# Attention into a mixture of attention experts on one core: v's blocks in pairs, q/k products by halves, a bound on loads, a new order

## The chip, the core and the metric

The kernel runs on one core of a Trainium2 chip. The metric is the device time in microseconds, from the first to the last instruction and what lies around it; several runs are made and the median is told. Five engines work side by side: TensorE (PE: matmuls; PEld: its weight loads), VectorE (DVE), ScalarE (ACT), GpSimd (POOL) and SyncE (SP), which here only issues DMAs. TensorE writes to eight PSUM banks of 512 fp32 columns; VectorE and ScalarE read them out.

## The reference

For 8 batches of 8 heads, 576 tokens and a head size of 64:

```python
kv  = einsum('bhsd,bhse->bhde', k, v)          # 64 x 64 a head, no softmax
out = einsum('bhsd,bhde->bhse', q, kv)
x   = out / sqrt(mean(out*out, -1) + 1e-6) * g_norm   # then heads side by side: 576 x 512
logits = x @ w_gate                             # 4 experts, the best 2 kept
w = softmax over the kept two
for e in range(4):                              # head size 64
    q, k, v = x @ wq[e], x @ wk[e], x @ wv[e]
    a = causal softmax(q @ k.T / 8)
    y += w[:, e] * (a @ v @ wo[e])              # zero where e isn't kept
```

## The kernel before

Each batch goes through the same steps, and eight batches are interleaved. A step is a named task (name, batch, index); `emit` maps names to functions:

- `lk`, `lv`, `lq` load k, v and q; k and v come in four pieces a batch (256 or 320 KB), q in two (576 KB). `lw`, `lwo` load weights, `ws`, `wo` bring them into their final type. `st` stores a block of the result.
- `kv` (L400) multiplies k and v, `kvc`, `kvx` bring the result into SBUF, `qc` transposes q (L423), `o` (L436) multiplies both. `oc` and `sq` copy and square o, `ms` (L468) sums squares, `ln`, `rs`, `na`, `nb`, `lo` (L487 to L506) make the reciprocal root, `bc` (L549) spreads it over the heads, `xm` (L557) multiplies it in: x, transposed, in `xT`.
- `G`, `L`, `lt` and the small tasks to `gate` choose the experts and their weights.
- `qp`, `kp` (`proj`, L629) multiply x by wq and wk for a pair of experts: two halves of 288 tokens into two banks, which one copy (`qpc`, `kpc`) brings out as 576 columns. `v` (L609) does one block of 128 tokens, 256 columns of one bank; `vc` copies it.
- `sc` (L659), `exp` (L671), `msk` (L678) make the weights of attention, `pv` (L704) multiplies them with v, `rc`, `iv`, `oc2` scale (L732), `ot` (L747) transposes, `y` (L777) is the last product, four matmuls of 256 columns a block; `yc` copies it to a stage buffer.

The order of the 1086 tasks is written out by hand as a string, `ORDER`, two characters a task. Two further strings give each task's engine (`ENGINE`) and the banks or buffers that it takes (`SLOTS`). Every engine and every DMA queue runs its tasks in that order. `place` hands out slots, `big` two banks, `small` one; `use` makes an instruction wait for other engines' work on its bank. `ZEROS` puts products of zeros (L812) ahead of some tasks at the start, so that TensorE is busy while the first loads come. All loads and, but for one task, all stores are issued on SyncE's queue, and a DMA there also waits for the eighth before it, whose semaphore it takes over.

```python
ZEROS = {
    ("kv", 0, 2): 31, ("kv", 0, 0): 14, ("o", 0, 0): 3,
}
```

Of the kernel before, what the change touches and what calls it, by code (L numbers as in the profile page):

```python
# [17 lines left out]
RUN, LO = 9, 4  # L18

# [6 lines left out]
    ("kv", 0, 2): 31, ("kv", 0, 0): 14, ("o", 0, 0): 3,  # L26
# [15 lines left out]
    "6PBJAEC+9u8IBKCy9VEqAFBMCzBN9xD4D5BLD6F4EuEv8H9X8G9YEwD8AIExAGDCDADDD7DBEy9+ACF1D9AH9Z9rADDE9sBU8J2OF3DFAM6X6Y"
    "DGBV9f8KC9DHBeBfEzDIBcE+9a8L9z8M9hBmF2CABnF0DJBdBW9b9y9c80E-6U9iBk6VBlBXC7DLC881DWBoDQDXALAJ9gDS8NDTDRDKBpBwDM"
    "Bs8OBxDUAKBtDVF6F54SFDDN6ZF7F8FBDOBuANBvFCA0F9AOFE8bA1BiA2APDsA3BqFAAQDPBYCDBj8cDtCBFFCC8PDYA46R8QCEEDBZ8SBaCJ"
    "Br6S6TC0DqA58TFGFHFIEBBzEEECDgByBgARDrFJB+FKCFDbBbBhFTFRASFLCGFUCMFSCHFM6QDyFX8R6WDZB-DaCIFNDzDhFOC1FPELDcFYCN"
    "CLC2DwC3EJEMC48YDxATEK8ZDmFQDd8UAUDnCKDuFVFWDvEFC58VC6COAWFrCPCQEGAX8WFsFtFl2RDoFuCRFmFvE0EREHD+CSDpCTD-EPE38a"
    "2LAcFwEIAVFZEOGIGJFcDkAYDlE2CaCUAdFa4PAZCbCVDiGKCgE1DjAeAa8dE4CcDeF-EQENGLCWFzFbChGQG0FdFxF+DfFy8XE52UFjFkFhG1"
    "E6FeESE7G2FfG3E84YGSGRGTCi4MFiGOAbFgETGMEUEVGNCdG6E9GWGYGUCeEWCXGPFnGVGXEAFpGZG7FoEXG8CYEeEfEYG5FqCfG9GaGEG4Gb"
    "EZCZEgGcEbGFGdGhEcGeEhEaEiGfGAEdGiGBGCGoGgGlGjGpGDGmEjGGGkGrGHGuGxGqGsGnGvGtGyGwGz"
)  # L50
ENGINE = (
    "SSSSSSSSSSGGVSASVSASVSVSVSVSAVVVVAAGAGAVAAAVVVVVVVAAAVAAAVAAAVVVAAAVVVGVVVVVVVVVVVVVGAGGVVGVAVAVAVVVAVVVVVAVAV"
    "AVAGGGGGVVGVVVVAVAVAVAVAVAGGGGGVVGVVAVVSVASVASVASSSSSSSSSSSVVVVAGGGAVVVVVVAGAAVAAGVAAAVVVVVVVGVVVVVVVVVGAVGVVG"
    "VAVAVAVVVVVAVVVAVAVAVAGGGGGVVGVVAVVVVVAVAVAVAGGGGGVVGVVAVVSVVSVASVASVASSSSSSSSSSSVVVVAVGGAVVVVVVVGAGAGVAVAAAVV"
    "VGVVVGVVVVVVVVVGAVGVVGVAVVVAVVVAVVVAVAVAVAVAGGGGGVVGVVAVAVVVAVAVAVAGGGGGVVGVVVVVSVVSVVSVVSSSSSSSSSSSVVVVVGVGGV"
    "VVVVVAGVAAAVGVAAAVVVVVVVGVVVVVVVVVGAGGVVGVVVVVAVAVVVVVAVAVAVAVAGGGGGVVGVVVVVVAVAVAVAVAGGGGGVVGVVAVVSVVSVVSVVSV"
    "ASSSSSSSSSSSVVVVAVAAVVVVVVVAGVGAGVGVAAAVVVVVVVGVVVVVVFVVGAVGVVGVAVAVVVAVAVVVVVAVAVAVAGGGGGVVGVVVVAVVVAVAVAVAGG"
    "GGGVVGVVVVASVASVASVVSSSSSSSSSSSVVVVVAAVAVVVVVVAGVGVGAAVAAAVVVGVVVGVVFVFVVVVGAGGVVGVAVAVVVAVVVAVAVAVAVAVAGGGGGV"
    "VGVVVVAVVVAVAVAVAGGGGGVVGVVVVASVVSVASVVSVVSSSSSSSSSSSVVVVAGGGVVVVVVVVAAGVAAAVAAAVVVGVVVVFVFVVVFVVGAVGVVGVAVAVV"
    "VAVVVAVAVAVAVAVAGGGGGVVGVVVVAVVVAVAVAVAGGGGGVVGVVVVASVASVASVASSSSSSSSSSSVVVVAAGVGVVVVVVVGVGAAAAVAAAVVVGVVVGVVV"  # L60
    "VVVVVVGAVGVVGVVVAVAVAVVVAVAVAVAVAVAGGGGGVVGVVVGVVAVVVAVAVAVAVAVAGGGGGVVGVVVGVVVVVVASVASVASVASVAC"
)
SLOTS = (
    "00001112345101674500134123201451672334401235601561201301150675341670015023016767230145607231601245236701452310"
    "16745101234200015603470156123456017012306745101236700145001016723401231415640167235012367454123010456723456701"
    "10014532671423014567013200456712450345110234510670234510672301452306101234567230014256000751546721234267010567"
    "06120045673074506701234856701452367014235601456011023041156722306945067234567106723450167234560123670011451670"
    "2310145016235A67B012235101134675013467501230456702390B451267301234506806745067340125011673660B0453567019456712"
    "301067023450001123637024509250113704253023502983530573"
# [13 lines left out]
def names(nb):  # L83
# [3 lines left out]
    for b in range(nb):  # L87
# [12 lines left out]
        out += [(m, b, i) for i in r5 for m in ("v", "vc")]  # L100
        for p in r2:
            out += [(m, b, p) for m in ("qp", "qpc", "kp", "kpc")]
# [3 lines left out]
        out += [(m, b, i) for i in (r5 if b % 2 else r4) for m in ("y", "yc", "st")]  # L106
# [14 lines left out]
def kernel(  # L121
# [37 lines left out]
    begun = [0]  # L159

# [154 lines left out]

    def load(m, dst, src, b, p, z):
        n, t0 = LO + z, LO * z
        hs = slice(4 * p, 4 * p + 4)
        rows = src[b, hs].rearrange("h (r t) d -> r h (t d)", t=RUN)[:, :, t0 * Dh : (t0 + n) * Dh]
        queue((m, b, p, z)).dma_start(dst[z::2, hs, 0:n, :].rearrange("r h t d -> r h (t d)"), rows)  # L320
# [13 lines left out]
    def lq(b, u):  # L334
        nc.sync.dma_start(
            q_t(b)[:, 2 * u : 2 * u + 2].rearrange("i m t d -> i m (t d)"),
            q[b, 4 * u : 4 * u + 4].rearrange("(m a) (i t) d -> (a i) m (t d)", a=2, t=RUN),
        )
# [22 lines left out]
    def lw(nm, p):  # L361
        queue(("lw", nm, p)).dma_start(
            stage(("x", nm, p))[:].rearrange("p c t -> p (c t)").rearrange("p (m f) -> p m f", f=Hd),
            w_dram[nm][2 * p : 2 * p + 2].rearrange("e (n p) f -> p (e n) f", p=P),
        )
# [11 lines left out]
    def lwo(_, pr):  # L377
        t = stage(("x", "wo", pr))
        nc.sync.dma_start(t[:].rearrange("p c t -> p (c t)"), moe_wo[2 * pr : 2 * pr + 2].rearrange("two d m -> (two d) m"))
# [226 lines left out]
    def v_mm(b, i):  # L606
        (n,) = small("v", b, i)
        for c in range(NCH):
            use(nc.tensor.matmul(  # L609
                bank(n)[:, 0 : E * Hd],  # L610
# [6 lines left out]
    def v_copy(b, i):  # L617
        nt = blocks[i][1]
        (n,) = small("v", b, i)
        use(copy(  # L620
            ("vc", b, i), vexts[b % 2][:nt, i, :, 0:Hd],
            bank(n)[:nt, 0 : E * Hd].rearrange("p (e f) -> p e f", e=E),
        ), n)

    def proj(nm, b, pr):
        ns = big(nm, b, pr)
        for s in range(2):
            for c in range(NCH):
                use(nc.tensor.matmul(  # L629
                    bank(ns[s])[:, 0:HALF],  # L630
                    lhsT=w_r[nm][:, c, 2 * pr : 2 * pr + 2, :].rearrange("p e f -> p (e f)"),
                    rhs=blocks_of(xTs[b % 2], c)[:, s * HALF : (s + 1) * HALF],
                    start=(c == 0),
                    stop=(c == NCH - 1),
                ), ns[s])
# [5 lines left out]
    def q_proj_copy(b, pr):  # L641
        proj_copy(("qpc", b, pr), buf(("qTp", b, pr), [P, S], FP32R, "qTp"))

    def k_proj_copy(b, pr):
        proj_copy(("kpc", b, pr), kTs[(2 * b + pr) % 3])
# [125 lines left out]
    def y_mm(b, qc):  # L771
        (n,) = small("y", b, qc)
        at = NF * P if qc == NF else b % 2 * (S + REM) + qc * P
        for a in range(2):
            for pr in range(EP):
                cols = slice(a * D // 2, (a + 1) * D // 2)
                use(nc.tensor.matmul(  # L777
                    bank(n)[:, cols], lhsT=OT[:, pr, at : at + P], rhs=wo_b[:, pr, cols],
                    start=(pr == 0), stop=(pr == EP - 1), skip_group_check=True,
                ), n)  # L780

    def y_copy(b, qc):
# [68 lines left out]
```

## Time and profile before

| | |
|---|---|
| median of 3 runs | 205.47 us (205.15 to 207.17) |
| profiled execution | 203.79 us |
| its span, first to last instruction | 202.0 us |
| TensorE busy | 193.4 us, 96% of the span |
| VectorE, ScalarE, GpSimd busy | 134.6, 128.1, 71.8 us |
| moved by DMA | 40.33 MB, 200 GB/s over the span |
| granted TensorE clock | 0.994 |

The profile's times are microseconds from the span's start. A line such as `L629 PE MATMUL banks<-xT,wq_r 128*128 128x288 f32 x128 | 20.3, 302 | 0.0` tells source line, engine, operation, what it writes and reads, its shape and count, busy time, the mean of one in ns, and the engine's idle time ahead of it with what ended that. Matmuls overlap, so that the mean of one is longer than the pace at which they follow each other; the pace is read from the chain of waits, where `81.05 0.98 PE banks L777 x8` is start, length, and eight matmuls. A matmul of fp32 that is no fp32r stands as two records. "issue" is time in which an engine waited for nothing that the profile shows.

### The profile page before, as it was taken

What the parts mean: (1) busy time and instruction counts of PE and PEld (TensorE: products, weight loads), DVE (VectorE), ACT (ScalarE), POOL (GpSimd) and SP (SyncE); (2) the same over time, 40 slices, a digit from 0 to 9 for tenths busy, and PEclk for the clock granted to TensorE, in tenths of its full rate; (3) what the DMA queues carried; (4) which work ended last, traced back from release to release, by engine and by line L of the source; (5) the groups of instructions that cost most, each with busy time, mean ns of one, the idle gap of its engine ahead of it and who ended that gap; (6) DMA issues with size and microseconds to landing.
All of it is one profiled execution on the core that took longest, in us unless ns stands there. A gap on an engine that the chain in (4) does not pass through costs nothing.

```text
span 202.0 us, 7288 instructions
## 1 busy us (share of the span) xinstructions
PE 193.4 (96%) x3040; PEld 160.1 (79%) x3040; DVE 134.6 (67%) x329; ACT 128.1 (63%) x229; POOL 71.8 (36%) x186
## 2 busy tenths in 40 slices
PE   7999999999999899999998999999999999999990
PEld 7996667888787687798965889779969778999880
DVE  7144699897759399973786788576667586444750
ACT  2026777666884578627946455896567858789572
POOL 8201043013917424471238420653305432343510
PEclk9999999999999999999999999999999999999997
DMA  4999979999996999500798401001000171509777
GB/s 151 281 356 357 331 179 256 307 340 379 366 336 225 346 375 366 191 3 5 212 351 308 133 28 55 5 3 55 0 3 5 43 269 49 215 19 311 248 278 246
DMA packets 33665, 40.33 MB, mean 200 GB/s; under 512 B 8272, under 2 KB 24672, under 8 KB 33632
## 3 DMA queue, kind: packets, MB, share of 16 engines
q1 hardware_dynamic: 33376, 39.59, 59.1%
q8 instruction: 24, 0.39, 0.8%
q10 hardware_dynamic: 160, 0.26, 0.5%
q0 software_dynamic: 96, 0.01, 0.1%
q14 instruction: 9, 0.07, 0.1%
HBM read 30.42 MB, written 9.44 MB: 197 GB/s over the span
## 4 chain that ended last, share of the span: by engine, by line
PE 88%; DVE 4%; ACT 3%; issue 2%; POOL 0%; DVEq 0%; POOLq 0%
PE banks L629 17%; PE banks L609 9%; PE banks L436 9%; PE banks L659 9%; PE banks L400 9%; PE banks L704 8%; PE banks L468 8%; PE banks L777 7%; PE banks L812 7%; PE banks L747 3%; PE banks L549 3%; PE banks L531 1%; ACT stage L304 1%; DVE osc L732 1%; DVE xT L557 1%
## 5 line engine op out<-in xcount | busy, mean ns | idle before, releaser
L671 ACT ACTIVATE PT<-banks 128x1024 bf16<-128x1024 f32 (+1 forms) x64 | 51.3, 838 | 10.8 <-PE banks L659 10.0
L678 POOL TENSOR_SCALAR_AFFINE_SELECT PT<-PT 128x256 bf16<-128x256 bf16 (+1 forms) x80 | 28.8, 380 | 21.6 <-ACT PT L671 21.3
L423 DVE STREAM_TRANSPOSE qT<-q_b 128x576 f32<-128x576 f32 x32 | 23.8, 760 | 8.3 <-DMA q_b<-in_q_dram 7.6
L460 POOL TENSOR_TENSOR sqs<-ob 128x576 f32<-128x576 f32 x17 | 19.3, 1144 | 20.4 <-DVE ob L305 14.5
L557 DVE TENSOR_TENSOR xT<-banks,ob 128x576 fp32r<-128x576 f32 x32 | 23.1, 747 | 2.4 <-PE banks L549 1.7
L609 PE MATMUL banks<-wv_r,xT 128*128 128x256 f32 x160 | 24.1, 287 | 0.0
L659 PE MATMUL banks<-qTp,kT 64*128 64x320 f32 (+3 forms) x224 | 21.8, 309 | 0.4 <-DVE ob L305 0.3
L609 PEld LDWEIGHTS banks<-wv_r,xT 128*128 128x128 f32 x160 | 20.6, 188 | 1.1 <-DVE wv_r L375 0.7
L400 PEld LDWEIGHTS banks<-v_b,k_b 128*64 128x64 f32 x640 | 19.6, 138 | 2.2 <-issue 1.3
L400 PE MATMUL banks<-v_b,k_b 128*64 128x64 f32 x640 | 21.1, 224 | 0.0
L777 PE MATMUL banks<-wo_b,OT 128*128 128x256 bf16 x144 | 20.6, 274 | 0.0
L659 PEld LDWEIGHTS banks<-qTp,kT 64*128 64x128 f32 x224 | 15.7, 185 | 5.9 <-issue 1.5
L629 PE MATMUL banks<-xT,wq_r 128*128 128x288 f32 x128 | 20.3, 302 | 0.0
L629 PE MATMUL banks<-xT,wk_r 128*128 128x288 f32 x128 | 19.7, 297 | 0.0
L436 PE MATMUL banks<-qT,kvs 32*64 32x288 f32 x256 | 19.5, 411 | 0.2 <-DVE qT L423 0.2
L704 PEld LDWEIGHTS <-PT 128*128 128x128 bf16 x480 | 15.9, 97 | 4.6 <-issue 1.8
L704 PE MATMUL banks<-vext,PT 128*128 128x65 bf16 x480 | 17.7, 193 | 1.7 <-issue 1.6
L436 PE MATMUL banks<-qT,kvm 32*64 32x288 f32 x256 | 18.6, 410 | 0.0
L629 PEld LDWEIGHTS banks<-xT,wq_r 128*128 128x128 f32 x128 | 17.5, 188 | 0.8 <-issue 0.4
L629 PEld LDWEIGHTS banks<-xT,wk_r 128*128 128x128 f32 x128 | 17.6, 188 | 0.1
L304 ACT COPY ob<-banks 128x576 f32<-128x576 f32 x17 | 10.6, 638 | 9.3 <-PE banks L436 8.2
L305 DVE COPY ob<-banks 128x576 f32<-128x576 f32 x15 | 11.3, 751 | 7.6 <-PE banks L436 4.2
(96 smaller groups left out, 308.8 us busy)
## 6 DMA issues: line engine op xcount, KB each, us to landing
q_b<-in_q_dram SPq DMA_DIRECT2D x16, 576.0 KB, 7.7
out_dram<-stage SPq DMA_DIRECT2D x32, 256.0 KB, 2.6
v_b<-in_v_dram SPq DMA_DIRECT2D x16, 320.0 KB, 7.5
k_b<-in_k_dram SPq DMA_DIRECT2D x16, 320.0 KB, 7.0
k_b<-in_k_dram SPq DMA_DIRECT2D x16, 256.0 KB, 6.8
v_b<-in_v_dram SPq DMA_DIRECT2D x16, 256.0 KB, 7.7
out_dram<-stage SPq DMA_DIRECT2D x6, 128.0 KB, 3.7
stage<-in_moe_wk_dram SPq DMA_DIRECT2D x2, 256.0 KB, 8.4
```

Of the source, the lines that this page charges most:

```text
L400: use(nc.tensor.matmul(p_kv[hh * Dh : (hh + 1) * Dh, c, :], lhsT=k_t(b)[:, h, j, :], rhs=v_t(b)[:, h, j, :], start=(j == 0), stop=(j == LO ...
L423: nc.vector.transpose(q_part(b, dh)[:, ms].rearrange("p m (t i) -> p m t i", t=RUN), q_t(b)[:, ms, :, dh * 32 : (dh + 1) * 32],)
L436: use(nc.tensor.matmul(bank(n)[at : at + Dh, 0:HALF], lhsT=(kvs if z == dh else kvm)[b % 2][pp, m], rhs=q_part(b, dh)[pp, m], start=(dh == ...
L460: nc.gpsimd.tensor_tensor(out=dst, in0=kept, in1=kept, op=AluOpType.mult)
L557: use(nc.vector.tensor_tensor(out=xTs[b % 2][:, 0 : NCH * S].rearrange("p (n s) -> p n s", s=S)[:, cs, cols], in0=both(ns)[:, :, 0:HALF], ...
L609: use(nc.tensor.matmul(bank(n)[:, 0 : E * Hd], lhsT=blocks_of(xTs[b % 2], c)[:, i * P : (i + 1) * P], rhs=w_r["v"][:, c, :, :].rearrange(" ...
L629: use(nc.tensor.matmul(bank(ns[s])[:, 0:HALF], lhsT=w_r[nm][:, c, 2 * pr : 2 * pr + 2, :].rearrange("p e f -> p (e f)"), rhs=blocks_of(xTs ...
L659: use(nc.tensor.matmul(bank(ns[el])[:, o : o + hi - lo], lhsT=kTs[(2 * b + pr) % 3][pp, kb * P : (kb + 1) * P], rhs=tiles["qTp", b, pr][pp ...
L671: use(nc.scalar.activation(PTs[(2 * b + pr) % 3][:, :, 512 * j : 512 * j + o], both(ns)[:, :, 0:o], ACTF.Exp, scale=scale), *ns)
L678: nc.gpsimd.affine_select(out=d, in_=d, compare_op=AluOpType.is_ge, fill=0.0, base=0, pattern=[[0, 2], [1, w]], channel_multiplier=-1,)
L704: use(nc.tensor.matmul(heads[el][:, k_ * W1 : (k_ + 1) * W1], lhsT=PT[:, el, col : col + P], rhs=vexts[b % 2][:, kb, 2 * pr + el, :], star ...
L777: use(nc.tensor.matmul(bank(n)[:, cols], lhsT=OT[:, pr, at : at + P], rhs=wo_b[:, pr, cols], start=(pr == 0), stop=(pr == EP - 1), skip_gr ...
```

## The change

- `v` puts two blocks into one bank (columns 0 to 255 and 256 to 511), and `vc` copies them together: three copies a batch instead of five.
- `qp`, `kp`, `qpc`, `kpc` have one more index, the half of the tokens: one bank and one copy of 288 columns each.
- `y` takes all 512 columns in one matmul for each pair of experts, two a block. The last batch's block 3 alone is split into two halves of columns, each with its own product, copy and store.
- Loads of k, v and q of batches 2 to 7 wait until the fourth DMA before them (`FLIGHT`), counted over the main loads and stores, has landed.
- `ORDER`, `ENGINE`, `SLOTS` and `ZEROS` are new: 1137 tasks, two of them stores on ScalarE's queue (blocks 1 and the second half of 3 of the last batch, in place of block 4). The two-bank objects took adjacent banks in all 174 cases before; now there are 142, and 38 of them are adjacent.

```diff
+FLIGHT = 4
...
-    ("kv", 0, 2): 31, ("kv", 0, 0): 14, ("o", 0, 0): 3,
+    ("kv", 0, 2): 26, ("o", 0, 1): 9, ("kv", 0, 0): 4, ("o", 0, 0): 4,
...
+    def queued(task, ins):
+        if len(task) > 1 and task[0] in ("lk", "lv", "lq") and task[1] > 1:
+            tc.add_manual_dep(ins.ins, moved[-FLIGHT].name, order_only, reason="queue")
+        moved.append(ins.ins)
...
     def v_mm(b, i):
-        (n,) = small("v", b, i)
+        (n,) = small("v", b, i // 2)
+        at = i % 2 * E * Hd
         for c in range(NCH):
             use(nc.tensor.matmul(
-                bank(n)[:, 0 : E * Hd],
+                bank(n)[:, at : at + E * Hd],
...
-    def proj(nm, b, pr):
-        ns = big(nm, b, pr)
-        for s in range(2):
-            for c in range(NCH):
-                use(nc.tensor.matmul(
-                    bank(ns[s])[:, 0:HALF],
...
+    def proj(nm, b, pr, s):
+        (n,) = small(nm, b, pr, s)
+        for c in range(NCH):
+            use(nc.tensor.matmul(
+                bank(n)[:, 0:HALF],
...
     def proj_copy(task, t):
-        ns = big(task[0][0], *task[1:])
-        use(copy(task, t[:, 0:S].rearrange("p (s n) -> p s n", s=2), both(ns)[:, :, 0:HALF]), *ns)
+        (n,) = small(task[0][0], *task[1:])
+        s = task[3]
+        use(copy(task, t[:, s * HALF : (s + 1) * HALF], bank(n)[:, 0:HALF]), n)
...
-        for a in range(2):
-            for pr in range(EP):
-                cols = slice(a * D // 2, (a + 1) * D // 2)
-                use(nc.tensor.matmul(
-                    bank(n)[:, cols], lhsT=OT[:, pr, at : at + P], rhs=wo_b[:, pr, cols],
+        cols = y_cols(h)
+        for pr in range(EP):
+            use(nc.tensor.matmul(
+                bank(n)[:, 0 : cols.stop - cols.start], lhsT=OT[:, pr, at : at + P], rhs=wo_b[:, pr, cols],
```

On TensorE the start reads, before and after (z: products of zeros, as counted by `ZEROS`):

```
before  z31 kv0.2 kv0.3 z14 kv0.0 kv0.1 o0.1 z3 o0.0 ms0.1 ms0.0 kv1.0 kv1.1 bc0.1.0 bc0.1.1 kv1.2 kv1.3 G0 bc0.0.0 bc0.0.1 o1.0 lt0 kp0.0 ...
after   z26 kv0.2 kv0.3 z9 o0.1 z4 kv0.0 kv0.1 ms0.1 z4 o0.0 bc0.1.0 ms0.0 kv1.0 kv1.1 bc0.1.1 G0 bc0.0.0 bc0.0.1 kv1.2 kv1.3 lt0 kp0.0.1 ...
```

More of the change, by code (lines that the diff above doesn't have):

```diff
@@ L99, in names @@
         out += [(m, b) for m in ("m8", "sh", "ex", "mk", "gt", "den", "rd", "gate")]
-        out += [(m, b, i) for i in r5 for m in ("v", "vc")]
+        out += [("v", b, i) for i in r5] + [("vc", b, j) for j in range(3)]
         for p in r2:
-            out += [(m, b, p) for m in ("qp", "qpc", "kp", "kpc")]
+            out += [(m, b, p, s) for s in r2 for m in ("qp", "qpc", "kp", "kpc")]
             out += [(m, b, p, j) for j in r4 for m in ("sc", "exp")] + [("msk", b, p, kb) for kb in r5]
@@ L105, in names @@
             out += [(m, b, p) + g for g in groups_of(b, nb) for m in (("ot", "otc") if b in BY_PE else ("td", "tl"))]
-        out += [(m, b, i) for i in (r5 if b % 2 else r4) for m in ("y", "yc", "st")]
+        out += [
+            (m, b, i) + h for i in (r5 if b % 2 else r4) for h in (((0,), (1,)) if (b, i) == (nb - 1, NCH - 1) else ((),))
+            for m in ("y", "yc", "st")
+        ]
     return out
@@ L159 @@
     begun = [0]
+    moved = []
     def place(key, n=1):
@@ L378, in lwo @@
         t = stage(("x", "wo", pr))
-        nc.sync.dma_start(t[:].rearrange("p c t -> p (c t)"), moe_wo[2 * pr : 2 * pr + 2].rearrange("two d m -> (two d) m"))
+        queued(("lwo",), nc.sync.dma_start(
+            t[:].rearrange("p c t -> p (c t)"), moe_wo[2 * pr : 2 * pr + 2].rearrange("two d m -> (two d) m")
+        ))
     def wo(_, pr):
@@ L615, in v_mm, with v_copy, q_proj_copy, k_proj_copy @@
             ), n)
[L617 to L619 removed]
+    def v_copy(b, j):
+        nt, k_ = (P, 2) if j < 2 else (REM, 1)
+        (n,) = small("v", b, j)
         use(copy(
[L621 to L622 removed]
+            ("vc", b, j), vexts[b % 2][:nt, 2 * j : 2 * j + k_, :, 0:Hd],
+            bank(n)[:nt, 0 : k_ * E * Hd].rearrange("p (n e f) -> p n e f", n=k_, e=E),
         ), n)
[L625 to L645 removed]
+    def proj(nm, b, pr, s):
[3 more added lines that the diff above has]
+                bank(n)[:, 0:HALF],
+                lhsT=w_r[nm][:, c, 2 * pr : 2 * pr + 2, :].rearrange("p e f -> p (e f)"),
+                rhs=blocks_of(xTs[b % 2], c)[:, s * HALF : (s + 1) * HALF],
+                start=(c == 0),
+                stop=(c == NCH - 1),
+            ), n)
+    def proj_copy(task, t):
+        (n,) = small(task[0][0], *task[1:])
+        s = task[3]
+        use(copy(task, t[:, s * HALF : (s + 1) * HALF], bank(n)[:, 0:HALF]), n)
+    def q_proj_copy(b, pr, s):
+        proj_copy(("qpc", b, pr, s), buf(("qTp", b, pr), [P, S], FP32R, "qTp"))
+    def k_proj_copy(b, pr, s):
+        proj_copy(("kpc", b, pr, s), kTs[(2 * b + pr) % 3])
     HB = S - 2 * P
@@ L769, in turn_last, with y_cols, y_mm, y_stage @@
         )
-    def y_mm(b, qc):
-        (n,) = small("y", b, qc)
+    def y_cols(h):
+        return slice(h[0] * D // 2, (h[0] + 1) * D // 2) if h else slice(0, D)
+    def y_mm(b, qc, *h):
+        (n,) = small("y", b, qc, *h)
         at = NF * P if qc == NF else b % 2 * (S + REM) + qc * P
-        for a in range(2):
-            for pr in range(EP):
-                cols = slice(a * D // 2, (a + 1) * D // 2)
-                use(nc.tensor.matmul(
-                    bank(n)[:, cols], lhsT=OT[:, pr, at : at + P], rhs=wo_b[:, pr, cols],
-                    start=(pr == 0), stop=(pr == EP - 1), skip_group_check=True,
-                ), n)
-    def y_copy(b, qc):
-        (n,) = small("y", b, qc)
-        use(copy(("yc", b, qc), stage(("x", "y", b, qc))[:].rearrange("p c t -> p (c t)"), bank(n)), n)
-    def store(b, qc):
-        t = tiles["x", "y", b, qc][:].rearrange("p c t -> p (c t)")
+        cols = y_cols(h)
+        for pr in range(EP):
+            use(nc.tensor.matmul(
+                bank(n)[:, 0 : cols.stop - cols.start], lhsT=OT[:, pr, at : at + P], rhs=wo_b[:, pr, cols],
+                start=(pr == 0), stop=(pr == EP - 1), skip_group_check=True,
+            ), n)
+    def y_stage(b, qc, h):
+        cols = y_cols(h)
+        return stage(("x", "y", b, qc) + h)[:].rearrange("p c t -> p (c t)")[:, 0 : cols.stop - cols.start]
+    def y_copy(b, qc, *h):
+        (n,) = small("y", b, qc, *h)
+        t = y_stage(b, qc, h)
+        use(copy(("yc", b, qc) + h, t, bank(n)[:, 0 : t.shape[1]]), n)
+    def store(b, qc, *h):
+        t = y_stage(b, qc, h)
         if qc < NF:
-            queue(("st", b, qc)).dma_start(out[b, qc * P : (qc + 1) * P, :], t)
+            queued(("st",), queue(("st", b, qc) + h).dma_start(out[b, qc * P : (qc + 1) * P, y_cols(h)], t))
             return
         for a in range(2):
-            queue(("st", b, qc)).dma_start(out[b - 1 + a, NF * P : S, :], t[a * REM : (a + 1) * REM])
+            queued(("st",), queue(("st", b, qc)).dma_start(out[b - 1 + a, NF * P : S, :], t[a * REM : (a + 1) * REM]))
     emit = dict(
@@ L809, in zero_matmuls @@
         else:
-            at = big(*({"qp": ("q",), "kp": ("k",)}.get(n[0], (n[0],)) + n[1:]))[0]
+            at = big(*n)[0]
         for _ in range(count):
```

90 lines of the change are left out of this document (47 added, 43 removed).

## The prediction

> **What bounds the kernel now.** I read the page's parts 1, 2 and 4 first, then the chain of waits in order of time, the groups of instructions with their shapes kept apart, and the DMA view in short windows.
>
> ```profile
> PE 193.4 (96%) x3040; PEld 160.1 (79%) x3040; DVE 134.6 (67%) x329; ACT 128.1 (63%) x229; POOL 71.8 (36%) x186
> DMA  4999979999996999500798401001000171509777
> PE 88%; DVE 4%; ACT 3%; issue 2%; POOL 0%; DVEq 0%; POOLq 0%
> ```
>
> TensorE is the bound: 88% of the chain is its own work, and no other engine is near it. DMA is full in the first 16 slices (each 5.05 us) and again in slices 20 to 22, so loads can bind until about 80 us and hardly later. Time can therefore come or go in five places: the start, the rate of TensorE's own work, its gaps, the loads' supply up to 62 us, and the tail.
>
> The start, from the chain in order of time:
>
> ```profile
> 17.27 0.86 PE banks L812 x6
> 18.13 1.26 PE banks L436 x32
> ...
> 19.92 0.65 ACT sqs L456
> ...
> 22.15 0.50 ACT root L487
> ...
> 22.68 0.45 ACT hi L491
> ...
> 23.15 0.54 ACT root L495
> ...
> 23.72 0.45 DVE root L500
> ...
> 24.83 0.42 DVE lo L506
> 25.26 0.67 DVE xT L557
> ...
> 27.32 1.54 PE banks L436 x32
> 28.86 0.39 PE banks L531 x12
> ```
>
> L812 are filler products of zeros, L436 is o of batch 0's half 0 and, at 27.32, of batch 1. The normalisation of half 0 (L487 at 22.15 to L506) ends at 25.25; from 27.32 TensorE runs almost without gaps. The exceptions on the chain:
>
> ```profile
> 68.12 0.86 PE banks L704 x24
> 68.98 0.83 issue
> ...
> 109.98 0.77 issue
> ```
>
> Twice it stood inside one group of independent products, waiting for nothing visible. The tail, from the chain and the timeline:
>
> ```profile
> 196.36 1.06 ACT stage L304 x2
> ...
> 197.47 0.58 ACT stage L304
> ...
> 198.08 1.19 ACTq L792 DMA_DIRECT2D out_dram<-stage  x2
> ```
>
> Three last evictions queue on ScalarE alone, and then two stores are issued one behind the other on ScalarE's queue.
>
> **The change, part by part.** All sums are against the profiled execution: 203.79 us, span 202.0. It lies 1.68 us below the median of the runs shown (205.47), so I add the difference in us to the median.
>
> *Last product by 512 columns.* 36 blocks went by four matmuls of 256 columns; 35 of them now go by two of 512, and one by two of 256 for each half.
>
> ```profile
> L704 PEld LDWEIGHTS <-PT 128*128 128x128 bf16 x480 | 15.9, 97 | 4.6 <-issue 1.8 <-DVE ob L305 0.8 <-ACT PT L671 0.5
> ...
> L777 PEld LDWEIGHTS <-OT 128*128 128x128 bf16 x144 | 12.2, 98 | 3.1 <-issue 0.8 <-DVE g_rd L597 0.5 <-ACT PT L671 0.3
> ...
> 122.71 0.91 PE banks L704 x30
> ...
> 179.59 1.33 PE banks L777 x12
> ```
>
> The chain gives the pace: 1.33 / 12 = 111 ns for 256 columns, 0.91 / 30 = 30 ns for 65. The line through both has 0.42 ns a column and 3 ns fixed, so two matmuls fewer save 6 ns a block: **-0.2 us**, bounds 0 (columns alone count) and -7.9 (if weight loads of 98 ns set the pace and half of 0.44 us went in 36 blocks). I stay at the first end: each of L704's 30 products has a load of 97 ns and they still pass at 30 ns. [...]
>
> *v in pairs, q/k products by halves.* The columns that TensorE streams are the same. In the built order its changes between array shapes go from 107 to 109, each at most the drain of the slowest product (411 ns, o and sums): 0 to +0.8, I take **+0.2**. What changes is the evictions:
>
> ```profile
> L305 DVE CAST kT<-banks 128x576 fp32r<-128x576 f32 x8 | 6.0, 747 | 1.4 <-PE banks L609 0.6 <-PE banks L629 0.6
> L304 ACT CAST kT<-banks 128x576 fp32r<-128x576 f32 x8 | 5.1, 637 | 4.6 <-PE banks L629 4.6
> L518 DVE TENSOR_TENSOR lpart<-banks,rstd 128x288 f32<-128x288 f32 x8 | 3.5, 440 | 0.1
> L487 ACT ACTIVATE root<-banks,eps 128x288 f32<-128x288 f32 x7 | 3.5, 504 | 4.0 <-PE banks L468 4.0
> L304 ACT CAST vext<-banks 128x256 bf16<-128x256 f32 x22 | 8.1, 376 | 5.6 <-PE banks L609 5.4
> L304 ACT COPY stage<-banks 128x512 f32<-128x512 f32 x21 | 11.9, 590 | 4.3 <-PE banks L777 2.7 <-DMA out_dram<-stage 1.1 <-ACT stage L304 0.3
> L468 PE MATMUL banks<-sqs,ones 128*32 128x288 f32 x128 | 10.8, 411 | 0.0
> ```
>
> 32 copies of 576 columns (14 x 747 + 18 x 637 ns = 21.9 us) become 64 of 288 (29 on VectorE at 440, 35 on ScalarE at about 440, between 504 and half of 637: 28.2). 40 v copies (40 x 0.38 = 15) become 16 of 512 columns at 0.59 and 8 of 256 (12.5). Net +3.8 us over two engines that are busy 67% and 63%: hidden by their idle third, up to +3.8 if it isn't. In return a half is ready, and a bank free, 0.2 to 0.3 us sooner, and the 174 two-bank objects, all in adjacent banks so far, become 142 in any two.
>
> ```profile
> L659 PEld LDWEIGHTS banks<-qTp,kT 64*128 64x128 f32 x224 | 15.7, 185 | 5.9 <-issue 1.5 <-DVE ob L305 0.5 <-ACT PT L671 0.5
> L436 PEld LDWEIGHTS banks<-qT,kvs 32*64 32x64 f32 x256 | 10.5, 131 | 3.3 <-DVE xT L557 0.7 <-ACT PT L671 0.4 <-DVE qT L423 0.4
> ```
>
> The waits that evictions end here are 0.5 + 0.5 + 0.7 + 0.4 = 2.1 us. I take **-0.6**; bounds -2.1 and +2.1, since the new order can lose as much elsewhere.
>
> *New order at the start.* The first k/v products need the first four loads rather than five, and o of half 1 goes ahead of the second k/v products. But o of half 0 still needs the tenth load and two transposes on VectorE.
>
> ```profile
> 15.89 1.44 DVE L423 STREAM_TRANSPOSE qT<-q_b 128x576 f32<-128x576 f32 x2 [0.55 <-DMA q_b<-in_q_dram]
> ...
> L304 ACT COPY ob<-banks 128x576 f32<-128x576 f32 x17 | 10.6, 638 | 9.3 <-PE banks L436 8.2
> ```
>
> The same ten loads come first, so that load lands near 15.9 again. VectorE now has one k/v copy and two moves to do ahead of the last transpose, so o starts near 18.4 in place of 18.13, and its squares end near 20.9 (20.57 before). New is that half 1's normalisation is over by then. ScalarE then copies two o blocks (0.64 each) before L487: 22.2 + 0.50 + 0.45 + 0.54 = 23.7; VectorE's 0.45 + 0.42 end at 24.6, then come one xT, 0.44 for L518 (above) and two more xT: 24.6 + 3 x 0.67 + 0.44 = 27.1. There the first k product of batch 0 starts, with lt (0.39, L531) already done. Against 27.32 with lt still to come this is **-0.6**, bounds +0.5 (a filler group of 0.86 in the way) and -2 (all three xT in the shade of other work).
>
> *Bound on loads.* Loads of batches 2 to 7 now wait on SyncE's queue until the fourth DMA before them has landed; before, eight could be under way. Everything behind on SP waits too: later loads, for which k/v products and transposes of q wait, and stores, which free the stage buffers. The first store now stands among the loads, but those behind it feed products over 10 us later.
>
> ```profile
> k_b<-in_k_dram SPq DMA_DIRECT2D x1, 256.0 KB, 3.2
> ...
> k_b<-in_k_dram SPq DMA_DIRECT2D x2, 256.0 KB, 6.5
> ...
> DMA packets 8508, 9.72 MB, mean 324 GB/s; under 512 B 1533, under 2 KB 7354, under 8 KB 8501
> ...
> 63.51 2.48 PE banks L400 x80
> ```
>
> The first row (95 to 96 us) is a load into an empty queue, 3.2 us; the second (66 to 70 us) in a full one, 6.5; the third is the traffic from 32 to 62 us. Four loads of 288 KB in 3.3 us give 350 GB/s, about what flows now. In the new order nearly the same products stand ahead of the end of batch 4's k/v as before, where it came at 65.99 (last row), and the same loads stand ahead of that on the queue, so supply and demand keep their places to 1 to 2 us, and a loss of some per cent in supply shows for only a few tenths: **+0.4**, bounds 0 and +5 (landing in 4.0 us: 288 GB/s, a ninth less than 324 over 33 us is 3.7 us, or a fifth less than 350, 6.6; the lead of 1 to 2 us goes off).
>
> The bound also shortens what stands ahead of an instruction fetch.
>
> ```profile
> q8 instruction: 24, 0.39, 0.8%
> ```
>
> 24 fetches of 16 KB are about TensorE's 6080 instructions, and the two unexplained gaps lie in slices 14 and 22, where the DMA row above reads 9 and 8. Read as late fetches, the two gaps (0.83 + 0.77) go with a queue half as deep: I take three quarters, **-1.2**; bounds -1.6 and +0.8 (one more). [...]
>
> *Tail.* The last copies are shared by both engines, the last block goes in halves, and its stores leave from two queues: of the 0.58 us behind another copy and the second issue (half of 1.19) I take **-0.5**, bounds 0 and -1.2.
>
> Sum: -0.2 + 0.2 - 0.6 - 0.6 + 0.4 - 1.2 - 0.5 = -2.5: 201.3 profiled, **203.0** against the median.
>
> **The rivals.**
> *Loads starve TensorE (slower).* With four in flight the queue drains at each wait. Place: k/v products of batches 2 to 4, 40 to 66 us. It decides once a load with three ahead of it takes over 3.7 us to land, when the lead of 1 to 2 us is used up. For: DMA is full throughout. Against: 3.2 us for a lone one. Price at 4.0 us: +5, with the other terms 203.0 + 4.6 = 207.6.
> *Nothing comes of it.* The gaps aren't fetches or return elsewhere (+1.2), and more and shorter evictions wait in line as long as before (+0.6 to +1): 205. For: VectorE and ScalarE get 3.8 us more work in strict order. Against: a third of both is idle.
> *More than I allow.* All eviction waits (2.1) and both gaps (1.6) go, the start gains 2: -0.2 + 0.2 - 2.1 - 2 + 0 - 1.6 - 0.5 = -6.2, 199.3. For: every one stands on the chain. Against: new orders make their own gaps.
> *Weight loads set the pace of the last product:* -7.9, 195; against it stands the row of L704. [...]
> *The change doesn't do what it says:* o of half 0 waits for the same tenth load, so the start could keep its time, and adjacent banks may never have been what was lacking; its time is that of the second, in whose chance it is contained.
>
> **How the numbers follow.** Forecast 0.42, more than allowed 0.16, nothing 0.24, loads starve 0.16, weight loads 0.02. About 1% (2 us) is what a measurement here tells from no change. Faster by over 1%: most of the forecast's cases and all of the third and fourth: 0.56. Within 1%: the second and the weak end of the forecast: 0.26. Slower: loads, and a bad end of the second: 0.18. The range reaches from 199.6 (most of the third) to 207.2 (most of the starving).
>
> **What would show it.** In the profile after: the first k product near 27; no "issue" piece over 0.5 us inside a group of pv products; loads from 32 to 62 us landing in 3.3 to 4 us at 340 GB/s or more; k/v products of batches 2 to 4 with no idle time ended by a DMA; last copies on both engines. I am wrong if TensorE's gaps between 30 and 66 us are ended by DMA, if the gaps inside products return, or if waits for ScalarE and VectorE grow over 2.1 us.

## The result and the profile after

The changed kernel takes 293.74 us (median of 4 runs) against 205.53 for the kernel before (4 runs): a ratio of 1.426, interval 1.420 to 1.432. The forecast was 203.0, range 199.6 to 207.2. The profiled run took 294.49 us, its span is 292.8. Medians are of all runs, while a ratio leaves out runs that took over 1.5% longer than the fastest of their kernel, such as the one of 296.88 us here.

The page of after, parts 1, 2 and 4, to be read against the first rows of the prediction:

```profile
span 292.8 us, 7119 instructions
...
PE 226.7 (77%) x2946; PEld 171.8 (59%) x2960; DVE 132.3 (45%) x330; ACT 132.5 (45%) x238; POOL 75.5 (26%) x193
...
PE   8987897769978846886779686988678676665793
...
PEclk9997999787999969999979975799799997995579
...
PE 62%; ACT 18%; DVE 13%; issue 5%; ACTq 0%; DVEq 0%
```

VectorE and ScalarE do nearly the same work as before (132.3 and 132.5 us against 134.6 and 128.1). TensorE stands idle for 292.8 - 226.7 = 66.1 us where it was 8.6, and its own work takes 33.3 us longer, with a granted clock that falls to little over half in some slices. The loss has no one place: most of the 40 slices show it. ScalarE's part of the chain goes from 3% to 18%, VectorE's from 4% to 13%, and no DMA is on it. So no engine has become the bound; the engines wait for one another.

The view of waits tells for whom an engine waited (us in total, times, the longest). TensorE's products of after, the five longest rows, then the only row of before in which they wait for more than 0.2 us for an evicting engine once the start is over:

```profile
PE banks L674 <- ACT PT L686: 10.9, 11, 1.6
PE banks L563 <- DVE xT L571: 4.9, 6, 2.0
PE banks L674 <- DVE xT L571: 4.1, 4, 1.5
PE banks L643 <- ACT PT L686: 3.0, 4, 1.1
PE banks L450 <- ACT PT L686: 2.0, 1, 2.0
```

```profile
PE banks L659 <- DVE ob L305: 0.3, 1, 0.3
```

The same for ScalarE, after and then before:

```profile
ACT PT L686 <- PE banks L563: 20.0, 6, 7.2
ACT ob L311 <- PE banks L450: 16.5, 7, 8.0
...
ACT PT L686 <- PE banks L674: 12.8, 13, 2.0
```

```profile
ACT PT L671 <- PE banks L659: 10.0, 14, 2.1
```

The row `ACT PT L686 <- PE banks L563` is the clue. L686 is the exponential; it reads two banks that L674 (`sc`) has filled. In before it waits for those products alone (L659 there). In after it waits 20.0 us for L563 (`bc`), whose products it doesn't read. The chain of after between 163 and 174 us shows the same in order of time:

```profile
162.75 0.46 PE banks L674 x2
...
163.34 0.84 DVE osc L747
...
164.22 0.42 PE banks L563 x2
...
164.66 1.03 ACT PT L686
...
165.71 0.77 DVE xT L571
...
166.53 0.61 PE banks L794 x2
167.14 0.25 PE banks L674 x2
...
167.41 0.77 DVE xT L571
...
168.22 0.83 PE banks L674 x8
169.05 0.13 PE banks L563 x2
169.19 4.03 PE banks L414 x80
```

TensorE does two products, stops, another engine evicts, and so on in turn. And the 80 k/v products that took 2.48 us in before (L400, in the prediction's rows) take 4.03.

The theory, A: `both` gives an eviction its two banks as one strided slice, `banks[:, n0 : n1 + 1 : n1 - n0, :]`. In before n1 was always n0 + 1. In after, of 142 two-bank objects 38 lie in neighbouring banks and 104 are 2 to 7 banks apart. If the framework that sets the semaphores takes such a slice for the whole stretch from n0 to n1, every eviction also waits for products into the banks between, and these for the eviction. I call such a wait a range wait. In the built programs I counted the waits between TensorE and ScalarE or VectorE (either way) whose two instructions share no bank, but where one lies between the other's two: **88 in after, none in before**. The count takes the waits that stand on the product or eviction itself; some more stand on an instruction of their own just ahead of one, and with these after has 112, before still none. The rivals: B, the bound on loads; C, the new order with its smaller copies; D, that after reuses its banks too soon, or that banks far apart are slow to read in one instruction.

### The profile page after: what moved, and what is told of

Same layout as the page of the kernel before. It is cut to its first block, busy times and chain, and to the rows that moved or that the text cites. A ratio compares the mean times of both kernels' runs of the same rounds, so it can differ in the third digit from the quotient of the medians.

```text
span 292.8 us, 7119 instructions
## 1 busy us (share of the span) xinstructions
PE 226.7 (77%) x2946; PEld 171.8 (59%) x2960; DVE 132.3 (45%) x330; ACT 132.5 (45%) x238; POOL 75.5 (26%) x193
## 4 chain that ended last, share of the span: by engine, by line
PE 62%; ACT 18%; DVE 13%; issue 5%; ACTq 0%; DVEq 0%
PE banks L643 10%; ACT PT L686 9%; PE banks L450 8%; PE banks L414 7%; PE banks L674 7%; PE banks L624 6%; PE banks L482 6%; PE banks L719 6%; DVE xT L571 5%; PE banks L794 4%; PE banks L836 4%; ACT ob L311 3%; DVE osc L747 3%; PE banks L563 2%; DVE ob L312 2%
## 5 line engine op out<-in xcount | busy, mean ns | idle before, releaser
L686 ACT ACTIVATE PT<-banks 128x1024 bf16<-128x1024 f32 (+1 forms) x64 | 52.0, 837 | 61.7 <-PE banks L563 20.0
L674 PE MATMUL banks<-qTp,kT 64*128 64x320 f32 (+3 forms) x224 | 27.8, 335 | 18.5 <-ACT PT L686 10.9
L674 PEld LDWEIGHTS banks<-qTp,kT 64*128 64x128 f32 x224 | 18.8, 197 | 28.4 <-ACT PT L686 14.1
L450 PE MATMUL banks<-qT,kvs 32*64 32x288 f32 x256 | 25.5, 487 | 4.8 <-ACT PT L686 2.0
L624 PEld LDWEIGHTS banks<-wv_r,xT 128*128 128x128 f32 x160 | 23.6, 212 | 6.8 <-ACT PT L686 2.5
L643 PE MATMUL banks<-xT,wk_r 128*128 128x288 f32 x128 | 24.0, 322 | 2.6 <-ACT PT L686 1.7
L643 PE MATMUL banks<-xT,wq_r 128*128 128x288 f32 x128 | 23.8, 316 | 1.5 <-ACT PT L686 1.3
L450 PE MATMUL banks<-qT,kvm 32*64 32x288 f32 x256 | 23.2, 488 | 0.8 <-ACT ob L311 0.4
L474 POOL TENSOR_TENSOR sqs<-ob 128x576 f32<-128x576 f32 x13 | 14.8, 1145 | 33.5 <-DVE ob L312 27.8
L794 PE MATMUL banks<-wo_b,OT 128*128 128x512 bf16 (+1 forms) x60 | 18.6, 402 | 5.4 <-DVE xT L571 1.3
L737 POOL TENSOR_TENSOR inv<-inv,gate 128x10 f32<-128x10 f32 (+2 forms) x18 | 3.8, 212 | 65.9 <-DVE inv L733 63.6
```

The costliest lines, as they stand in the source:

```text
L450: use(nc.tensor.matmul(bank(n)[at : at + Dh, 0:HALF], lhsT=(kvs if z == dh else kvm)[b % 2][pp, m], rhs=q_part(b, dh)[pp, m], start=(dh == ...
L624: use(nc.tensor.matmul(bank(n)[:, at : at + E * Hd], lhsT=blocks_of(xTs[b % 2], c)[:, i * P : (i + 1) * P], rhs=w_r["v"][:, c, :, :].rearr ...
L643: use(nc.tensor.matmul(bank(n)[:, 0:HALF], lhsT=w_r[nm][:, c, 2 * pr : 2 * pr + 2, :].rearrange("p e f -> p (e f)"), rhs=blocks_of(xTs[b % ...
L674: use(nc.tensor.matmul(bank(ns[el])[:, o : o + hi - lo], lhsT=kTs[(2 * b + pr) % 3][pp, kb * P : (kb + 1) * P], rhs=tiles["qTp", b, pr][pp ...
L686: use(nc.scalar.activation(PTs[(2 * b + pr) % 3][:, :, 512 * j : 512 * j + o], both(ns)[:, :, 0:o], ACTF.Exp, scale=scale), *ns)
L794: use(nc.tensor.matmul(bank(n)[:, 0 : cols.stop - cols.start], lhsT=OT[:, pr, at : at + P], rhs=wo_b[:, pr, cols], start=(pr == 0), stop=( ...
```

## The experiments

Wait counts in this section are range waits that stand on the instruction itself, from the built programs. Times are medians; ratios are to before on the same chip.

**Neighbouring pairs in after (e1).** `SLOTS` alone is new, so that each two-bank object lies in two neighbours:

```diff
 SLOTS = (
-    "00000123411001145602135214023006732165437015624012456310753602711364507123100107451203641216072346150723154001"
+    "00001234511001126734150212734005631123445670123456023710502367415012367450100167123405021213674501236745231001"
...
```

> After with its banks dealt out anew so that each of the 142 two-bank objects lies in two neighbouring banks; order, engines, sizes, bound on loads as in after. Theory A (the instruction that evicts a two-bank object is ordered as if it touched every bank between its two, so that it waits for products of other objects and they for it; 88 such waits between TensorE and ScalarE or VectorE in the built program of after, none in before, none here): 200 to 208 us, the waits of ScalarE's exponentials for TensorE's other products gone. Rival B (the bound on loads starves TensorE): stays at 285 to 300. Rival C (the new order, with the q/k halves and v pairs, makes the engines wait for one another): stays at 285 to 300. Rival D (after reuses its banks too soon): 240 or less only if the new deal reuses later; medians of TensorE's work between two uses of a bank are 2.4 us here, 2.1 in after and before, so D expects little change, 270 to 295.

209.8 us, ratio 1.025 (1.019 to 1.031), the granted clock 0.998. The page, and the exponential's group:

```profile
PE 193.8 (93%) x2946; PEld 154.1 (74%) x2960; DVE 133.2 (64%) x330; ACT 131.5 (63%) x238; POOL 75.5 (36%) x193
...
L686 ACT ACTIVATE PT<-banks 128x1024 bf16<-128x1024 f32 (+1 forms) x64 | 51.3, 836 | 9.1 <-PE banks L674 7.7
```

84 of the 88 us are gone, with the bound, the order and all sizes of the change in place; most of the exponential's idle time is ended by L674 again, as in before. The time lies 1.8 us above A's range (200 to 208). B and C fall as causes of the bulk.

**Any pairs, dealt out by the same rule (e2).** As e1, but the rule may take any two banks; only `SLOTS` differs.

> After with its banks dealt out anew by the same rule of reuse as the run with neighbouring pairs (median 2.4 us of TensorE's work between two uses of a bank), but pairs in any two banks: 52 of 142 neighbouring, 90 apart by 2 to 7. 66 waits of the disputed kind. Theory A: 88 waits cost 88 us, about 1 us each, so 66 give 260 to 275. Rival D (reuse too soon): the same time as the run with neighbouring pairs, since reuse is the same. Rivals B and C: 285 to 300.

289.6 us, ratio 1.416 (1.404 to 1.427). The reuse of banks follows the rule of e1, so D's first half falls. The time lies above the 260 to 275 that I had expected: 66 waits cost 79.8 us over e1, 1.2 each, where I had assumed 1.0.

**Before with its banks renamed (e3, e10).** Nothing but the names of the eight banks:

```diff
 SLOTS = (   # e3: bank n becomes 0 4 1 5 2 6 3 7; e10: 0 2 1 3 4 6 5 7; a pair is written lower bank first
-    "00001112345101674500134123201451672334401235601561201301150675341670015023016767230145607231601245236701452310"
+    "00004111526104372600125145204261371534204153604361101501460376251370046015043737150426307151304226153704261510"
...
```

> Before with its banks renamed only: bank n becomes 0 4 1 5 2 6 3 7 for n = 0 to 7, so that its 174 neighbouring pairs lie 3 or 4 banks apart; the same objects share the same bank at the same times, order, engines, sizes and loads are before's. 158 waits of the disputed kind appear. Theory A: about 1 us each, 300 to 370 us. Rivals B, C and D: 205 us, as nothing they speak of is changed. A fourth thought, that one instruction reading two distant banks is slow in itself: about 205 plus at most a few us, with longer evictions in the groups.

> Before with its banks renamed only, 0 2 1 3 4 6 5 7 for n = 0 to 7: its 174 pairs now lie 1 (24) or 2 (150) banks apart. 81 waits of the disputed kind against 158 in the first renaming (+182 us). Theory A, by 1.0 to 1.2 us a wait: 285 to 300, with TensorE's mean granted clock near 0.88. If the distance itself counted and not the waits: near 205 to 230.

e3 takes 386.5 us, ratio 1.889 (1.876 to 1.903); e10 284.3 us, ratio 1.385 (1.368 to 1.402). The kernel before, with the same work in the same order, is slowed by 182 us by some 160 such waits, and by 79 us by some 80. e3 came out above its range and e10 just below: the sign and the order of size were right, the price of a wait isn't a constant. Whether a distant pair is slow to read is seen in the exponential's group, e3 first, then before:

```profile
L671 ACT ACTIVATE PT<-banks 128x1024 bf16<-128x1024 f32 (+1 forms) x64 | 52.6, 837 | 90.3 <-PE banks L659 27.3 <-PE banks L549 10.8 <-PE banks L629 5.7
```

```profile
L671 ACT ACTIVATE PT<-banks 128x1024 bf16<-128x1024 f32 (+1 forms) x64 | 51.3, 838 | 10.8 <-PE banks L659 10.0 <-DVE inv L718 0.4
```

One takes 837 ns from banks 3 or 4 apart and 838 from neighbours. What grew is the idle time ahead of it, 10.8 to 90.3 us, now ended by L549 and L629 too, which fill other banks. D's second half falls.

**After without the bound (e4).** The two lines of the condition in `queued` are left out.

> After without its bound on loads (loads of batches 2 to 7 no longer wait for the fourth DMA before them), all else as in after. Theory A: 288 to 296, as now. Rival B: 205 to 215. Rival C: 285 to 300.

293.8 us, ratio 1.436 (1.424 to 1.448), as after itself: the bound isn't seen at all behind the waits.

**After with split evictions (e9).** The banks stay where the change put them; a pair that isn't neighbouring is read by two instructions:

```diff
+    def parted(ns):
+        if ns[1] - ns[0] < 2:
+            return [(slice(0, 2), both(ns), ns)]
+        return [(slice(e, e + 1), banks[:, n : n + 1, :], (n,)) for e, n in enumerate(ns)]
...
-        use(nc.scalar.activation(
-            PTs[(2 * b + pr) % 3][:, :, 512 * j : 512 * j + o], both(ns)[:, :, 0:o], ACTF.Exp, scale=scale
-        ), *ns)
+        for e, t, n in parted(ns):
+            use(nc.scalar.activation(
+                PTs[(2 * b + pr) % 3][:, e, 512 * j : 512 * j + o], t[:, :, 0:o], ACTF.Exp, scale=scale
+            ), *n)
...
```

The same is done in `o_copy`, `square`, `xm`, `rc` and `o_scale`.

> After with its own banks, order, engines and bound on loads, but each two-bank object whose banks aren't neighbours (104 of 142) is evicted by two instructions of one bank each. No wait of the disputed kind is left between TensorE and the others, though the pairs lie where they lay. Theory A (the one instruction over both banks is ordered as if it touched those between): most of the 88 us goes; 104 more evictions at about 0.24 us each (2 x 440 for 637 ns) put some 25 us on ScalarE and VectorE, so 208 to 225. The rival that distant pairs are slow or badly placed in themselves: 285 or more, longer than after, since evictions are added.

206.9 us, ratio 1.008 (1.004 to 1.012). The page, and ScalarE's and TensorE's waits (the exponential is L695 here, `sc` L682, `kv` L419):

```profile
PE 193.1 (95%) x2960; PEld 154.9 (76%) x2960; DVE 136.5 (67%) x381; ACT 134.1 (66%) x300; POOL 75.6 (37%) x193
...
ACT PT L695 <- PE banks L682: 5.8, 13, 1.4
...
PE banks L419 <- DMA v_b<-in_v_dram: 0.9, 1, 0.9
```

The pairs lie as in after, none of the 88 waits is left, and 86.8 us go. The bank plan was good; reading it by one strided instruction was the fault. The time lies just under my range of 208 to 225, since my price for the added evictions was far too high: for 113 more instructions VectorE and ScalarE together have 5.8 us more work than in after, not 25.

**The rest, on neighbouring pairs (e5, e6, e7, e12).** e1 was still 5 us slower than before. In its trace GpSimd issues the load of g_norm (L354) at 17.78 us, where before has it (L342) at 4.87; the timeline of GpSimd, before, then e1:

```profile
4.87 1.22 POOL L342 DMA_DIRECT2D g_part<-in_g_norm_dram  x2
```

```profile
17.78 1.05 POOL L354 DMA_DIRECT2D g_part<-in_g_norm_dram  x2
24.02 2.99 POOL L387 TENSOR_SCALAR wk_r<-stage,g_part 128x256 fp32r<-128x256 f32 x3 [5.20 <-DMA g_part<-in_g_norm_dram]
```

This load and that of the gate's weights are the two that are not issued by SyncE. In the new `ORDER` its task stands behind the moves `kvx`, which wait for VectorE, and so GpSimd waits 5.20 us for it afterwards. e5 takes the bound away from e1, e6 puts the tasks `lwg` and `lgv` right behind the first load, e7 does both:

```diff
 ORDER = (   # e6 and e7
-    "06040705090V0W0Y0f010d0j03020B0e000g0k0m0r0T082b2e0U0X0a0u0H2c2d2g0s0c0-2i0Z0i0b100A2f2h110h0t2j122k0l0o0q1314"
+    "060B0A040705090V0W0Y0f010d0j03020e000g0k0m0r0T082b2e0U0X0a0u0H2c2d2g0s0c0-2i0Z0i0b102f2h110h0t2j122k0l0o0q1314"
...
-        if len(task) > 1 and task[0] in ("lk", "lv", "lq") and task[1] > 1:   # e5 and e7
-            tc.add_manual_dep(ins.ins, moved[-FLIGHT].name, order_only, reason="queue")
```

> After with neighbouring pairs (209.8 us) and besides without the bound on loads. It asks what of the 5 us by which that run is still slower than before comes from the bound. Rival B, as left for this rest (the bound keeps the loads of batches 3 and 4 on the path: DMA moved 218 to 295 GB/s from 40 to 70 us there, 277 to 362 in before): 206 to 207.5, with 320 GB/s or more. The other thought (the rest is the late load of g_norm and the new order's own gaps): 209 to 210.5.

> After with neighbouring pairs (209.8 us) and besides the two small loads of GpSimd's queue (the gate's weights and g_norm) put right behind the first load, ahead of the moves of k/v that wait on VectorE. In the run with neighbouring pairs g_norm is issued at 17.8 us and lands at 23.8, GpSimd waits 5.2 us for it and VectorE 2.9 (in before: issued at 4.9, no wait). If this late load is part of the rest, TensorE's idle time from 20 to 40 us (2.7 us more than in before) shrinks to about 1: 207.5 to 208.5. If TensorE's gaps there come from the order or the later halves: 209 to 210.5.

> After with neighbouring pairs, without the bound on loads and with the two small loads first: the two edits of the runs sent with it together. If both causes are real and act apart: 204 to 206, level with before (204.5) to a little over. If neither: 209 to 210.5. Rival C for the rest (the new order has its own gaps of 3 to 5 us): not under 207.

210.3 us (ratio 1.022, 1.017 to 1.028), 209.3 (1.018, 1.014 to 1.021) and 208.0 (1.013, 1.009 to 1.016). Singly they can't be told from e1; together they take back about half, less than the 204 to 206 that I had expected of two causes that act apart. e12 moves four tasks of e7 to other engines, ahead of exponentials that TensorE waits for:

```diff
 ENGINE: ("wo", "o", 1) and ("otc", 1, 0)  A -> V;  ("sq", 2, 1, 0)  A -> G;  ("ws", "k", 1)  V -> A
```

> The run with neighbouring pairs, unbound loads and g_norm first (208.0), with four tasks on other engines: the second cast of the output weights and one copy of OT from ScalarE to VectorE, one square from ScalarE to GpSimd, the second scaling of wk from VectorE to ScalarE. Each stands there ahead of an exponential, or of the scaling itself, for which TensorE waits (1.0, 1.1, 0.4 and 0.8 us). If the rest of 2.6 us is exponentials that stand behind other evictions on an engine that works in order: 205 to 207. If the gaps move elsewhere: 207.5 to 209.

208.7 us, ratio 1.019 (1.011 to 1.028): no gain; what makes e7's rest is left open. The change's own plan of banks does without it:

**The rest, on the change's own banks (e13, e14).** e9 with the two small loads first; then also without the bound.

> After with split evictions (206.9 us) and the two small loads of GpSimd's queue first; the bound on loads stays. TensorE's gaps in the run with split evictions: 3.0 us from 10 to 36 us (0.3 in before), and 0.9 at 68.2 us, ended by a load of v. If the late g_norm makes half of the first: 205 to 206. If the gaps at the start come from the order itself: 206.5 to 207.5.

> The same, and without the bound on loads. Theory: with the range waits, the late g_norm and the bound gone, nothing of the slowdown is left, and what else the change does (v pairs, halves of q/k, last product by 512, the order) is worth nothing or a little: 203 to 205.5, level with before. If the order and the sizes cost by themselves: 206 to 208.

205.8 us, ratio 1.001 (0.997 to 1.005), and **204.0 us, ratio 0.993 (0.989 to 0.997)**: with the waits, the late load and the bound gone, the change is faster than before, by about 0.7%. The medians of all runs, 12 and 23, lie 1.3 us apart. That is the best version found.

**One part on before each (e8, e11).** The last product by 512 columns (`for a in range(1)`, `cols = slice(0, D)` in `y_mm`), and the bound alone (`queued` of the change put around before's loads).

> Before with one part of the change alone: the last product by two matmuls of 512 columns a block in place of four of 256. The prediction's term: 0.2 us less (columns alone set the pace); its rival (weight loads set the pace of this product): up to 7.9 us less, 197. [...] I expect 204 to 205, and 200 to 220 ns from one product of 512 columns to the next.

> Before with the bound on loads alone (a load of batches 2 to 7 waits until the fourth DMA before it has landed). The prediction's term: 0.4 us, bounds 0 to 5. From the two pairs of runs with neighbouring banks (209.8 against 210.3, and 209.3 against 208.0): -0.5 to 1.3. I expect 205 to 207. Rival B: 208 or more.

e8: 205.6 us, ratio 1.001 (0.998 to 1.005), no change. e11: 207.4 us, ratio 1.011 (1.004 to 1.019), at the upper end of what I had expected. The chain of e8, TensorE's waits in e11 (`kv` is L408), and the stretch from 32 to 62 us of e11, then of before (TensorE, its loads, VectorE, ScalarE, GpSimd, clock, DMA share, GB/s):

```profile
191.24 0.86 PE banks L777 x4
```

```profile
PE banks L408 <- DMA k_b<-in_k_dram: 2.4, 1, 2.4
...
32.00:62.00 30.00, 28.66 (x453) 23.12 (x438) 22.50 (x52) 20.60 (x37) 9.05 (x19) 1.00 0.88 270
```

```profile
32.00:62.00 30.00, 29.66 (x476) 24.31 (x478) 23.60 (x52) 21.92 (x38) 10.57 (x22) 1.00 0.98 324
```

## Why the prediction was wrong

**The step that failed** is the eviction waits, -0.6 with bounds -2.1 and +2.1: "the 174 two-bank objects, all in adjacent banks so far, become 142 in any two". It was booked as a freedom. It was the cost: +87 us (after against e9), forty times the bound. The bound was taken from the eviction waits that before has, and such a row can't hold a wait that doesn't exist while no bank lies between a pair. Both halves of the warning stood in what the prediction had: the slice in `both`, unchanged by the diff, whose stretch is n1 - n0 + 1 banks, and the built programs, whose waits can be counted. The order of instructions was compared, their waits were not. The prediction's closing condition ("if waits for ScalarE and VectorE grow over 2.1 us") is the one that came true.

**Last product by 512 columns**, -0.2: e8 shows no change within about 1 us, and four products in 0.86 us are 215 ns each, about what the prediction's line gives for 512 columns (0.42 x 512 + 3 = 218). The rival of 195 us falls.

**Bound on loads**, +0.4 with bounds 0 and +5: right in kind and place, mis-sized. Alone on before it costs 1.1% (0.4 to 1.9), some 2.3 us, and the gap stands at the k/v products, ended by a load, where the rival of starving loads had put it. The step that failed in it is the 350 GB/s for four loads under way, landing in 3.3 us: e11 moves 270 from 32 to 62 us, before 324, and its loads of k and v there took 4.1 to 5.1 us. From e13 to e14 it is 1.8 us.

**Start**, -0.6 with bounds +0.5 and -2: wrong. The first k product comes at 31.99 us in after, at 29.7 in e9, 28.3 in e13 and 28.7 in e14, not at 27.1. Two terms were missed: the range waits, and the two small loads on GpSimd's queue, put behind `kvx`. From e9 to e13 these loads are worth 0.7% (ratios 1.008 and 1.001), about 1.4 us. The prediction had counted the queues of TensorE, ScalarE, VectorE and SyncE at the start, and not GpSimd's. A rest stays even without both: in e14 the second transpose of q ends at 18.9 us where the forecast had o start at 18.4, `lo` ends at 25.3 in place of 24.6, and the last xT at 28.1 in place of 27.1. What makes this rest is open.

**Late fetches**, -1.2: the reading is borne out, the cure isn't. TensorE's waits in e9 and e11 have no "issue" row, as forecast for a bound queue, and in e14, where the bound is gone, they are back:

```profile
PE banks L727 <- issue: 0.8, 1, 0.8
...
PE banks L417 <- issue: 0.5, 1, 0.5
```

But e1 and e6 have the bound and such waits of 0.6 and 1.8 us, so that the bound takes them away isn't shown. That they are fetches the traces make likely. The gaps of before stand behind 2242 and 3521 recorded instructions of TensorE, those of e8 behind 2242 and 3519, those of e1 and e6 behind 2241, those of e14 behind 705 and 2241: to within two records, these places lie multiples of 256 instructions apart. Each of these gaps ends 1.2 to 1.5 us after a fetch of 16 KB on queue q8 has landed; in before these land at 68.27 and 109.52 us, and the gaps end at 69.81 and 110.75. How long a fetch stood behind loads no record tells, so that no run shows the three quarters behind the -1.2. The one that landed at 68.27 took 0.94 us itself, with a DMA share of 1.00 from 65.7 to 70.7 us; six between 122 and 158 us took 0.92 to 1.11, with a share of 0.05 from 121 to 160.

**Tail**, -0.5 with bounds 0 and -1.2: not seen. The last products of before, from its timeline, then those of e14 with its last copies:

```profile
195.68 1.63 PE L777 MATMUL banks<-wo_b,OT 128*128 128x256 bf16 x12
```

```profile
194.27 1.62 PE L804 MATMUL banks<-wo_b,OT 128*128 128x512 bf16 x8
...
195.93 0.42 DVE L317 COPY stage<-banks 128x256 f32<-128x256 f32 x1 [0.23 <-PE banks L804]
195.98 0.59 ACT L316 COPY stage<-banks 128x512 f32<-128x512 f32 x1 [0.45 <-PE banks L804]
```

Both engines share the last copies, as forecast, and start as soon as the last products end, at 195.9; the span ends at 200.7, 4.8 us on. In before the last products end at 197.3 and the span at 202.0, 4.7 us on. So the 1.3 us that e14 gains in span lie ahead of the last products, and in which part is open.

**More and shorter evictions**, up to +3.8 us on two engines, hidden: nothing speaks against it. VectorE and ScalarE have 264.7 us of work in e1 and 262.7 in before, GpSimd 75.5 and 71.8; e14 has 270.8 on the two and is still no slower than before. The +0.2 us for changes between array shapes no run tells apart. In before, where TensorE isn't idle between the two, a product of another array shape starts a median of 216 ns after the one ahead of it, and at most 354, within the 411 that the term took as its bound; one of the same shape starts a median of 30 ns after it, most of these being products of 64 or 65 columns.

## What to carry to other kernels

A slice with a step over PSUM banks is ordered here as the whole stretch that it spans: after, with 88 such waits, took 293.7 us. So two banks that one instruction reads belong side by side (209.8 us, e1); where they can't, two instructions read them (206.9, e9). A plan that frees the banks must be judged by the waits of the built program, which can be counted before anything runs. A bound taken from the waits that a profile shows says nothing of waits that the present layout can't have. And an order written out anew moves the small loads on the least busy queue too: look for what now stands ahead of each.

## What the runs showed that I had not expected

A range wait cost about a microsecond on average in each of four comparisons: 182 us for some 160 (e3), 79 for some 80 (e10), 80 for 66 (e2 against e1), 87 for 88 (after against e9). With the waits that stand on instructions of their own, 204, 104, 89 and 112, it is 0.8 to 0.9 us each. One exponential takes 0.84 us, so that a price of one eviction for each wait would have told the size; that each wait lasts one eviction isn't shown.

The granted clock was lower in each run with range waits, where TensorE works in short bursts without any long pause: 0.911 in e10, 0.896 in e4, 0.894 in after, 0.875 in e2 and 0.776 in e3. It was 0.998 in e1, and came back with the waits gone (0.999 in e9). From 174 to 180 us of after, as in the rows of windows above:

```profile
174.00:180.00 6.00, 2.74 (x31) 1.44 (x40) 1.75 (x4) 2.96 (x4) 1.65 (x5) 0.67 0.25 90
```

Of after's 90.8 us of span over before, 57.5 are idle time of TensorE and 33.3 longer work. The clock's record of after stands at 0.5 for 62.2 us, in which TensorE is busy for 50.5. Products of x by wv follow each other there every 213 ns (median), and every 118 at full clock; those of `pv` every 55 and every 29. At the pace of full clock that work would take some 22 to 24 us less, by this estimate about 70% of the 33.3. The longest gap between TensorE's products is 2.0 us in after and 2.8 in e3; after has 77 gaps of over 0.1 us between products, before 7. What in the waits lowers the clock these runs don't tell.
